# Feed-forward products on float32 operands instead of three float32r products on split operands, in an attention and feed-forward kernel

## The chip, the core and the metric

The kernel runs on one core of a Trainium2 chip. Its engines work side by side and meet through semaphores: TensorE (PE in the profile, its weight loads PEld) multiplies matrices, VectorE (DVE) and ScalarE (ACT) work on elements, GpSimd (POOL) too, and SyncE (SP) issues transfers. The metric is the time of one execution on the device in microseconds. The profile is of one execution and names instructions by engine and by the line of the kernel.

## The reference

The input is q, k and v of 8 batches, 8 heads, 576 positions and 64 features in float32. Attention is within chunks of 64 positions; its output becomes tokens of 512 features, which pass through a normalization and a feed-forward layer of 2048 hidden features (FFN):

```python
scores = scale * np.matmul(q_c, k_c.transpose(0, 1, 2, 4, 3))
scores = scores - np.max(scores, axis=-1, keepdims=True)
attn = np.exp(scores)
attn = attn / (np.sum(attn, axis=-1, keepdims=True) + 1e-09)
out = np.matmul(attn, v_c)
...
xn = (x - mu) / np.sqrt(var + 1e-06) * g_ln
ch = np.maximum(xn @ w_ch1, 0.0) @ w_ch2
return (x + ch).astype(np.float32)
```

The two weight matrices arrive as 64-bit floats.

## The kernel before

There are 4608 tokens, taken in 18 pairs of 128 (256 tokens a pair). Two pairs make a tile of 512 tokens, and there are 9 tiles.

Attention (function attention, once per pair). SP loads q and k and, later, v. PE makes the scores in 32 matmuls of 64x64 by 64 (line 159), float32, each in one of the four 64x64 quarters of the array (r is the half of the rows, c the half of the columns). DVE takes the maxima (166) and subtracts them (172), ACT takes the exponentials (176). The result is transposed, for the first four pairs by PE against an identity (191), for the others by DVE in blocks of 32 (204). PE multiplies by v in 32 more float32 matmuls (216), DVE divides (224) and takes mean and variance (234, 235), and after line 239 the tokens are transposed again, by PE (255) or DVE (267), so that features stand on the partitions.

FFN (function ffn). The weights are 16 blocks, each of 128 hidden features: 512 columns of the first matrix and 512 of the second. For a tile, up(f) makes 128 hidden features of all its tokens: four products over the 512 input features into one bank h (294). ACT applies ReLU (304). down(f) adds their share to the outputs y, one bank for each 128 tokens (317), and after the last block DVE adds the tokens (326) and SP stores them. Most products have 512 columns on the moving side; the first two tiles work for their first six blocks on single pairs, with 256 columns in up.

Precision. TensorE gets float32r operands there, which hold fewer bits than float32. So every operand is kept as two float32r tiles, the rounded value and the rest: weights wh and wl, tokens xth and xtl, activations hh and hl. A product is three matmuls, high by high, high by rest, rest by high. The rests are made by DVE: wl at line 113, hl at 305, xtl at 248 (for the first four pairs; by POOL on the same line for the others).

Weights (function convert_w, letter w in the order). A half block of 64-bit words (raw, 512 KB, line 81) is loaded; there are three buffers. ACT and four DVE instructions (89, 96, 97, 100, 104) turn it into float32 in place, ACT writes wh (108), DVE writes wl (113). After round i come the rest of half block i-1 and the load of half block i+2. There are 32 half blocks, and all are converted within the first 130 us.

Order. No scheduler decides it: the strings START, STEADY and LAST list, letter by letter, which stream (attention of a pair, FFN of a tile, conversion of weights) takes its next step, and each engine executes its instructions in that order. In the steady part PE gets up(f+1) and then down(f), so that ReLU and the rest of block f+1 have a down(f) to hide behind.

Of the kernel before, what the change touches and what calls it, by code (L numbers as in the profile page):

```python
# [7 lines left out]

F32 = mybir.dt.float32
BF16 = mybir.dt.bfloat16  # L10
F32R = mybir.dt.float32r
U32 = mybir.dt.uint32
U64 = mybir.dt.uint64
AF = mybir.ActivationFunctionType
ALU = mybir.AluOpType
AX = mybir.AxisListType

P = 128
B, H, S, D = 8, 8, 576, 64
DM = H * D  # L20
DFF = 4 * DM
T = B * S
PAIR = 2 * P
# [3 lines left out]
NK = DM // P  # L27
NF = DFF // P
NW = 2 * DM
HALF = NW // 2  # L30
RAW_AHEAD = 3
# [19 lines left out]
def chunk_attention_ffn(ctx: ExitStack, tc: tile.TileContext, qkv, g, w, out):  # L51
    nc = tc.nc
    PSUM = bass.MemoryType.PSUM

    const = ctx.enter_context(tc.tile_pool(name="const", bufs=1))
# [3 lines left out]
    xtp = ctx.enter_context(tc.tile_pool(name="xt", bufs=2))  # L59
    hp_ = ctx.enter_context(tc.tile_pool(name="hp", bufs=2))  # L60
# [9 lines left out]
    nc.gpsimd.memset(mhalf, -0.5)  # L70
    g_sb = const.tile([P, DM], F32, name="g_sb")

    wh = [const.tile([P, NW], F32R, name=f"wh{i}") for i in range(NF)]
    wl = [const.tile([P, NW], F32R, name=f"wl{i}") for i in range(NF)]

    stage, converted = {}, set()

    def fetch_w(i):
        if i < 2 * NF:
            raw = raw_pool.tile([P, HALF], U64, name="raw")  # L80
            nc.sync.dma_start(raw, w[i // 2, :, (i % 2) * HALF : (i % 2 + 1) * HALF])
            words = raw.bitcast(U32).rearrange("p (n two) -> p n two", two=2)
            stage[i] = words[:, :, 0], words[:, :, 1]

    def start_w(i):
        if i < 2 * NF:
            lo, hi = stage[i]
            wf = raw_pool.tile([P, HALF], F32, name="wf", bufs=1)
            nc.scalar.activation(wf, hi.bitcast(F32), AF.Abs)  # L89
            stage[i] = lo, hi, wf  # L90

    def round_w(i):

        lo, hi, wf = stage[i]
        wu = wf.bitcast(U32)
        nc.vector.tensor_scalar(out=wf, in0=wf, scalar1=F64_LOW, scalar2=F64_HIGH, op0=ALU.max, op1=ALU.min)
        nc.vector.tensor_scalar(  # L97
            out=wu, in0=wu, scalar1=0x07FFFFFF, scalar2=3, op0=ALU.bitwise_and, op1=ALU.logical_shift_left
        )
        nc.vector.scalar_tensor_tensor(  # L100
            out=lo, in0=lo, scalar=29, in1=wu, op0=ALU.logical_shift_right, op1=ALU.bitwise_or
        )
        start_w(i + 1)
        nc.vector.scalar_tensor_tensor(  # L104
            out=lo, in0=hi, scalar=0xC0000000, in1=lo, op0=ALU.bitwise_and, op1=ALU.bitwise_or
        )
        f, cs = i // 2, slice((i % 2) * HALF, (i % 2 + 1) * HALF)
        nc.scalar.copy(wh[f][:, cs], lo.bitcast(F32))

    def split_w(i):  # L110
        wf = stage.pop(i)[0].bitcast(F32)
        f, cs = i // 2, slice((i % 2) * HALF, (i % 2 + 1) * HALF)
        nc.vector.tensor_tensor(out=wl[f][:, cs], in0=wf, in1=wh[f][:, cs].bitcast(F32), op=ALU.subtract)  # L113
        converted.add(i)

    def convert_w():

        for i in range(RAW_AHEAD):
            fetch_w(i)
        yield  # L120
        start_w(0)
        yield
        for i in range(2 * NF):
            round_w(i)
            if i > 0:
                split_w(i - 1)
                fetch_w(i - 1 + RAW_AHEAD)
            yield
        split_w(2 * NF - 1)
        yield  # L130

    def attention(pair, xt_cols, xs, by_pe):
# [20 lines left out]
        for j in range(2):  # L153
            for a in range(HP):
                for h2 in range(2):
                    r = slice(h2 * D, (h2 + 1) * D)
                    for c in range(2):
                        cs = slice(j * P + c * D, j * P + (c + 1) * D)
                        nc.tensor.matmul(  # L159
                            s[h2][c * D : (c + 1) * D, j * HP + a, :], lhsT=q_t[r, a, cs], rhs=k_t[r, a, cs],  # L160
                            start=True, stop=True,
# [9 lines left out]
        for h2 in range(2):  # L171
            nc.vector.tensor_tensor(
                out=p_sb[:, :, h2, :], in0=s[h2], in1=top[:, :, h2 : h2 + 1].broadcast_to([P, 2 * HP, D]),
                op=ALU.subtract,
# [48 lines left out]
        for h2 in range(2):  # L223
            nc.vector.tensor_tensor(
                out=x_h[:, :, h2, :], in0=o[h2], in1=rden[:, :, h2 : h2 + 1].broadcast_to([P, 2 * HP, D]),
                op=ALU.mult,
# [14 lines left out]
            )  # L241
        yield

        xth, xtl = xt_cols()

        def rest(on, j, xt):
            js = slice(j * P, (j + 1) * P)
            on.tensor_tensor(out=xtl[:, :, js], in0=xt, in1=xth[:, :, js].bitcast(F32), op=ALU.subtract)  # L248

        if by_pe:  # L250
            xt = []
            for j in range(2):
                xt.append(bank().rearrange("p (k t) -> p k t", k=NK))
                for k in range(NK):
                    nc.tensor.transpose(out=xt[j][:, k, :], in_=xg[:, j, k * P : (k + 1) * P], identity=ident)
                nc.scalar.copy(xth[:, :, j * P : (j + 1) * P], xt[j])  # L256
                if j == 0:
                    yield
                    rest(nc.vector, 0, xt[0])
            yield  # L260
            rest(nc.vector, 1, xt[1])
        else:
            xt = work.tile([P, 2 * NK, P], F32, name="xt", tag="work")
            xg = xg.rearrange("p j (k t) -> p (j k) t", k=NK)
            for j in range(4):
                for i in range(4):
                    nc.vector.transpose(out=xt[quad(j), :, quad(i)], in_=xg[quad(i), :, quad(j)])  # L267
                yield
            for j in range(2):
                nc.scalar.copy(xth[:, :, j * P : (j + 1) * P], xt[:, j * NK : (j + 1) * NK, :])  # L270
                rest(nc.gpsimd, j, xt[:, j * NK : (j + 1) * NK, :])
        vare = small.tile([P, 2], F32, name="vare")
        nc.vector.tensor_scalar_add(vare, mv[:, :, 1], 1e-6)
        rstd = small.tile([P, 2], F32, name="rstd", bufs=6)
# [4 lines left out]
    def ffn(first, n, xt, xs, fs, last):  # L279

        nt = n * PAIR
        slots = DM // nt
        held = []
        f0, f1 = fs
        y = []

        def up(f):
            assert 2 * f in converted and all(first + i in xs for i in range(n))
            h = ps_h.tile([P, nt], F32, name="h")
            xth, xtl = xt()  # L290
            m = 0
            for k in range(NK):
                for wx, x in ((wh, xth), (wh, xtl), (wl, xth)):
                    nc.tensor.matmul(  # L294
                        h, lhsT=wx[f][:, k * P : (k + 1) * P], rhs=x[:, k, :], start=m == 0, stop=m == 3 * NK - 1
                    )
                    m += 1
            return h

        def split(f, h):  # L300
            if f % slots == 0:
                held[:] = [hp_.tile([P, slots, nt], F32R, name=f"h{i}") for i in "hl"]
            hh, hl = (x[:, f % slots, :] for x in held)
            nc.scalar.activation(hh, h, AF.Relu)  # L304
            nc.vector.scalar_tensor_tensor(  # L305
                out=hl, in0=h, scalar=0.0, in1=hh.bitcast(F32), op0=ALU.max, op1=ALU.subtract
            )
            return hh, hl

        def down(f, hh, hl):  # L310
            assert 2 * f + 1 in converted
            if f == f0:
                y.extend(ps_y.tile([P, DM], F32, name="y") for _ in range(2 * n))
            for j in range(2 * n):
                js = slice(j * P, (j + 1) * P)
                for m, (hx, wx) in enumerate(((hh, wh), (hh, wl), (hl, wh))):
                    nc.tensor.matmul(  # L317
                        y[j], lhsT=hx[:, js], rhs=wx[f][:, DM:],
                        start=f == f0 and m == 0, stop=f == f1 - 1 and m == 2,
                    )  # L320

        def finish():
            for j in range(2 * n):
                pair, jj = first + j // 2, j % 2
                x, rstd = xs[pair]
                nc.vector.scalar_tensor_tensor(  # L326
                    out=x[:, jj, :], in0=y[j], scalar=rstd[:, jj : jj + 1], in1=x[:, jj, :], op0=ALU.mult, op1=ALU.add
                )
                if last:
                    row = pair * PAIR + jj * P  # L330
                    nc.sync.dma_start(out[row : row + P, :], x[:, jj, :])

        hs = {}

        def products():
            hs[f0] = up(f0)
            yield
            for f in range(f0, f1):
                if f + 1 < f1:
                    hs[f + 1] = up(f + 1)  # L340
                    yield
                down(f, *hs.pop(f))
                hs["done"] = f + 1
                yield

        def rectified():
            for f in range(f0, f1):
                hs[f] = split(f, hs[f])
                yield
            assert hs["done"] == f1  # L350
            finish()
            yield

        return products(), rectified()
# [9 lines left out]
    class Tokens:  # L364
# [4 lines left out]

        def cols(self, i, n=1):  # L370
            if not self.x:
                self.x.extend(xtp.tile([P, NK, 2 * PAIR], F32R, name=f"xt{c}") for c in "hl")
            return [x[:, :, i * PAIR : (i + n) * PAIR] for x in self.x]

        def attention(self, i, by_pe):
            return attention(2 * self.t + i, lambda: self.cols(i), xs, by_pe)
# [54 lines left out]
```

## Time and profile before

| | us |
|---|---|
| median of 2 runs | 899.92 (899.84 to 900.0) |
| the profiled execution | 899.33 |
| its span, first to last instruction | 897.6 |
| PE busy in the span | 853.5 |
| DVE busy | 568.3 |
| ACT busy | 173.3 |
| POOL busy | 48.3 |

The granted TensorE clock is 0.997 of full speed over the span. The groups of the page that the change touches are, in us busy: matmuls of line 294 in three groups of 624 each, 236.6, 233.9 and 234.0; of line 317 in three groups of 576 each, 226.0, 224.4 and 224.4; on DVE line 305 with 101.2; on POOL line 248 with 35.6.

How to read such rows: a group has its line, engine, operation, output and inputs by name, shapes, the number of instructions, then busy time and mean duration, and behind the second bar the idle time of the engine before them and who ended it. For a matmul, "128*128 128x512" is the weights' size and the output's. Matmuls overlap, so their durations add up to more than the time they take; the distance of two starts is the rate.

### The profile page before, as it was taken

The numbers are of one execution on the slowest core, as the hardware profiler recorded it, in microseconds if no ns is written. First come the engines' busy times: TensorE is split into PE (matmuls) and PEld (weight loads), VectorE is DVE, ScalarE is ACT, GpSimd is POOL, SyncE is SP. The second block draws the span as 40 slices with busy tenths as digits, with TensorE's granted clock in tenths as the row PEclk, the third lists the DMA queues.
The fourth block names the chain that finished last, engine by engine and source line by source line (L and its number), as shares of the span: only waits on it lengthen the run. The fifth ranks groups of instructions, "written<-read, shape, count | busy, mean of one in ns | idle before, by whom it ended". The sixth has DMA issues, their size and how long they took to land.

```text
span 897.6 us, 14036 instructions
## 1 busy us (share of the span) xinstructions
PE 853.5 (95%) x5968; PEld 706.5 (79%) x5968; DVE 568.3 (63%) x1104; ACT 173.3 (19%) x301; POOL 48.3 (5%) x53
## 2 busy tenths in 40 slices
PE   2379999999999999999999999999999999999998
PEld 2368888888888788878888888888888888888886
DVE  5988887788876566656565656565666565661112
ACT  3343433412111111121212021212011111111110
POOL 0000000001000000010101010101010101010000
PEclk9999999999999999999999999999999999999999
DMA  6544153212030103010301030103010220000001
GB/s 220 191 145 161 62 175 118 94 48 71 1 135 8 48 0 119 24 47 1 119 24 47 1 118 24 47 1 117 25 47 1 72 71 1 1 30 19 0 1 47
DMA packets 20367, 55.70 MB, mean 62 GB/s; under 512 B 2256, under 2 KB 2256, under 8 KB 20304
## 3 DMA queue, kind: packets, MB, share of 16 engines
q1 hardware_dynamic: 20160, 54.53, 17.4%
q8 instruction: 47, 0.77, 0.4%
q10 hardware_dynamic: 144, 0.26, 0.1%
q14 instruction: 16, 0.13, 0.0%
HBM read 45.35 MB, written 9.44 MB: 61 GB/s over the span
## 4 chain that ended last, share of the span: by engine, by line
PE 89%; DVE 6%; DMA 2%; ACT 1%; issue 1%; SPq 0%; DVEq 0%; ACTq 0%
PE h L294 44%; PE y L317 41%; PE s L159 2%; PE s L216 2%; DMA k_t<-qkv 1%; DVE pt_sb L204 1%; DMA raw<-w 1%; DVE raw L100 1%; DVE raw L104 1%; DVE x L326 1%; DVE hl L305 1%; ACT hh L304 1%; DVE wf L97 0%; DVE top L166 0%; DVE wl L113 0%
## 5 line engine op out<-in xcount | busy, mean ns | idle before, releaser
L305 DVE SCALAR_TENSOR_TENSOR hl<-h,hh 128x512 fp32r<-128x512 f32 (+1 forms) x156 | 101.2, 650 | 264.8 <-ACT hh L304 264.6
L294 PE MATMUL h<-xth,wh 128*128 128x512 f32 (+1 forms) x624 | 236.6, 379 | 0.7 <-ACT xth L256 0.7
L294 PE MATMUL h<-xth,wl 128*128 128x512 f32 (+1 forms) x624 | 233.9, 375 | 3.0 <-DVE wl L113 3.0
L294 PE MATMUL h<-xtl,wh 128*128 128x512 f32 (+1 forms) x624 | 234.0, 375 | 1.1 <-DVE xtl L248 1.1
L317 PE MATMUL y<-wh,hh 128*128 128x512 f32 x576 | 226.0, 392 | 2.1 <-ACT hh L304 2.0
L317 PE MATMUL y<-wl,hh 128*128 128x512 f32 x576 | 224.4, 390 | 0.0
L317 PE MATMUL y<-wh,hl 128*128 128x512 f32 x576 | 224.4, 390 | 0.0
L304 ACT ACTIVATE hh<-h 128x512 fp32r<-128x512 f32 (+1 forms) x156 | 87.8, 564 | 582.5 <-PE h L294 578.9
L294 PEld LDWEIGHTS h<-xth,wl 128*128 128x128 f32 x624 | 118.6, 190 | 23.9 <-DVE wl L113 3.2
L294 PEld LDWEIGHTS h<-xth,wh 128*128 128x128 f32 x624 | 118.5, 190 | 23.2 <-ACT xth L256 1.1
L294 PEld LDWEIGHTS h<-xtl,wh 128*128 128x128 f32 x624 | 118.5, 190 | 22.0 <-DVE xtl L248 1.4
L317 PEld LDWEIGHTS y<-wh,hh 128*128 128x128 f32 x576 | 108.2, 188 | 25.1 <-ACT hh L304 3.0
L317 PEld LDWEIGHTS y<-wh,hl 128*128 128x128 f32 x576 | 108.1, 188 | 23.4 <-DVE hl L305 0.9
L317 PEld LDWEIGHTS y<-wl,hh 128*128 128x128 f32 x576 | 108.2, 188 | 21.5
L204 DVE STREAM_TRANSPOSE pt_sb<-p_sb 32x256 f32<-32x256 f32 x224 | 97.7, 436 | 5.2 <-ACT p_sb L176 1.4
L267 DVE STREAM_TRANSPOSE xt<-xg 32x256 f32<-32x256 f32 x224 | 97.6, 436 | 3.5
L248 POOL TENSOR_TENSOR xtl<-xt,xth 128x512 fp32r<-128x512 f32 x28 | 35.6, 1290 | 644.8 <-ACT xth L270 416.0
L326 DVE SCALAR_TENSOR_TENSOR x<-y,rstd,x 128x512 f32<-128x512 f32 x44 | 30.6, 749 | 15.3 <-PE y L317 15.2
L166 DVE TENSOR_REDUCE top<-s 128x8 f32<-128x512 f32 x36 | 23.2, 686 | 24.4 <-PE s L159 24.4
L89 ACT ACTIVATE wf<-raw 128x512 f32<-128x512 f32 x32 | 21.8, 683 | 76.5 <-DMA raw<-w 53.8
L159 PE MATMUL s<-k_t,q_t 64*64 64x64 f32 x1152 | 22.6, 231 | 14.1 <-DMA k_t<-qkv 14.1
L159 PEld LDWEIGHTS s<-k_t,q_t 64*64 64x64 f32 x1152 | 20.0, 144 | 19.2 <-issue 11.1
(35 smaller groups left out, 383.7 us busy)
## 6 DMA issues: line engine op xcount, KB each, us to landing
raw<-w SPq DMA_DIRECT2D x32, 512.0 KB, 3.6
q_t<-qkv SPq DMA_DIRECT2D x18, 512.0 KB, 4.2
k_t<-qkv SPq DMA_DIRECT2D x18, 512.0 KB, 5.4
v_t<-qkv SPq DMA_DIRECT2D x36, 256.0 KB, 3.1
out<-x SPq DMA_DIRECT2D x36, 256.0 KB, 2.1
g_sb<-g ACTq DMA_DIRECT2D x1, 256.0 KB, 4.5
```

The costliest lines, as they stand in the source:

```text
L89: nc.scalar.activation(wf, hi.bitcast(F32), AF.Abs)
L159: nc.tensor.matmul(s[h2][c * D : (c + 1) * D, j * HP + a, :], lhsT=q_t[r, a, cs], rhs=k_t[r, a, cs], start=True, stop=True,)
L166: nc.vector.tensor_reduce(out=top[:, :, h2], in_=s[h2], axis=AX.X, op=ALU.max)
L204: nc.vector.transpose(out=pt_sb[quad(2 * h2 + j), :, c, quad(i)], in_=p_sb[quad(2 * c + i), :, h2, quad(j)])
L216: nc.tensor.matmul(o[h2][c * D : (c + 1) * D, j * HP + a, :], lhsT=pt_sb[r, j * HP + a, c, :], rhs=v_t[j][r, a, c, :], start=True, stop=True,)
L248: on.tensor_tensor(out=xtl[:, :, js], in0=xt, in1=xth[:, :, js].bitcast(F32), op=ALU.subtract)
L267: nc.vector.transpose(out=xt[quad(j), :, quad(i)], in_=xg[quad(i), :, quad(j)])
L294: nc.tensor.matmul(h, lhsT=wx[f][:, k * P : (k + 1) * P], rhs=x[:, k, :], start=m == 0, stop=m == 3 * NK - 1)
L304: nc.scalar.activation(hh, h, AF.Relu)
L305: nc.vector.scalar_tensor_tensor(out=hl, in0=h, scalar=0.0, in1=hh.bitcast(F32), op0=ALU.max, op1=ALU.subtract)
L317: nc.tensor.matmul(y[j], lhsT=hx[:, js], rhs=wx[f][:, DM:], start=f == f0 and m == 0, stop=f == f1 - 1 and m == 2,)
L326: nc.vector.scalar_tensor_tensor(out=x[:, jj, :], in0=y[j], scalar=rstd[:, jj : jj + 1], in1=x[:, jj, :], op0=ALU.mult, op1=ALU.add)
```

## The change

FFN products are one matmul each, on operands of type float32. The second copies fall away: wl, xtl and hl, and with them the instructions that made them. The weights stay in one set of tiles ws, to which the last of the four DVE instructions writes directly; the ACT copy of line 108 is gone. Tokens are one tile xt, the activations one tile h, written by ReLU. The load of a half block is issued after each round, of half block i+3 instead of i+2. The strings of the order are untouched.

```diff
-    wh = [const.tile([P, NW], F32R, name=f"wh{i}") for i in range(NF)]
-    wl = [const.tile([P, NW], F32R, name=f"wl{i}") for i in range(NF)]
+    ws = [const.tile([P, NW], F32, name=f"ws{i}") for i in range(NF)]
...
         nc.vector.scalar_tensor_tensor(
-            out=lo, in0=hi, scalar=0xC0000000, in1=lo, op0=ALU.bitwise_and, op1=ALU.bitwise_or
+            out=ws[f].bitcast(U32)[:, cs], in0=hi, scalar=0xC0000000, in1=lo, op0=ALU.bitwise_and, op1=ALU.bitwise_or
         )
-        nc.scalar.copy(wh[f][:, cs], lo.bitcast(F32))
-
-    def split_w(i):
-        wf = stage.pop(i)[0].bitcast(F32)
-        nc.vector.tensor_tensor(out=wl[f][:, cs], in0=wf, in1=wh[f][:, cs].bitcast(F32), op=ALU.subtract)
...
             round_w(i)
-            if i > 0:
-                split_w(i - 1)
-                fetch_w(i - 1 + RAW_AHEAD)
+            fetch_w(i + RAW_AHEAD)
...
-                nc.scalar.copy(xth[:, :, j * P : (j + 1) * P], xt[:, j * NK : (j + 1) * NK, :])
-                rest(nc.gpsimd, j, xt[:, j * NK : (j + 1) * NK, :])
+                nc.scalar.copy(xt_[:, :, j * P : (j + 1) * P], xt[:, j * NK : (j + 1) * NK, :])
...
             for k in range(NK):
-                for wx, x in ((wh, xth), (wh, xtl), (wl, xth)):
-                    nc.tensor.matmul(
-                        h, lhsT=wx[f][:, k * P : (k + 1) * P], rhs=x[:, k, :], start=m == 0, stop=m == 3 * NK - 1
-                    )
-                    m += 1
+                nc.tensor.matmul(
+                    h, lhsT=ws[f][:, k * P : (k + 1) * P], rhs=x[:, k, :], start=k == 0, stop=k == NK - 1
+                )
...
             nc.scalar.activation(hh, h, AF.Relu)
-            nc.vector.scalar_tensor_tensor(
-                out=hl, in0=h, scalar=0.0, in1=hh.bitcast(F32), op0=ALU.max, op1=ALU.subtract
-            )
...
-                for m, (hx, wx) in enumerate(((hh, wh), (hh, wl), (hl, wh))):
-                    nc.tensor.matmul(
-                        y[j], lhsT=hx[:, js], rhs=wx[f][:, DM:],
-                        start=f == f0 and m == 0, stop=f == f1 - 1 and m == 2,
-                    )
+                nc.tensor.matmul(y[j], lhsT=hh[:, js], rhs=ws[f][:, DM:], start=f == f0, stop=f == f1 - 1)
```

PE in the steady part, before, at the end of an up and the start of a down (h and y are the PSUM banks, the numbers behind wh and wl count the weight tiles):

```order
L294 MATMUL h<-xth,wh_108 128x512
L294 MATMUL h<-xtl,wh_108 128x512
L294 MATMUL h<-xth,wl_124 128x512
L317 MATMUL y<-wh_107,hh 128x512
L317 MATMUL y<-wl_123,hh 128x512
L317 MATMUL y<-wh_107,hl 128x512
```

and at the same place after the change:

```order
L273 MATMUL h<-xt,ws_108 128x512 x4
L291 MATMUL y<-ws_107,h 128x512 x4
L273 MATMUL h<-xt,ws_109 128x512 x4
L291 MATMUL y<-ws_108,h 128x512 x4
L273 MATMUL h<-xt,ws_110 128x512 x4
```

An up and a down had 12 matmuls each and have 4 each; the order among them is the same.

DVE at the second half block of weights (raw words, wf the scratch tile) and the denominators of the first attention, before:

```order
L96 TENSOR_SCALAR wf<-wf 128x512
L97 TENSOR_SCALAR wf<-wf 128x512
L100 SCALAR_TENSOR_TENSOR raw<-raw,wf 128x512
L104 SCALAR_TENSOR_TENSOR raw<-raw 128x512
L113 TENSOR_TENSOR wl_112<-raw,wh_96 128x512
L182 TENSOR_REDUCE den<-p_sb 128x16
```

and after:

```order
L94 TENSOR_SCALAR wf<-wf 128x512
L95 TENSOR_SCALAR wf<-wf 128x512
L98 SCALAR_TENSOR_TENSOR raw<-raw,wf 128x512
L103 SCALAR_TENSOR_TENSOR ws_96<-raw 128x512
L171 TENSOR_REDUCE den<-p_sb 128x16
```

Each round of the weights has four DVE instructions in place of five.

SP's first transfers, before:

```order
L137 DMA k_t<-qkv 128x1024
L81 DMA raw<-w 128x512 x3
L169 DMA v_t<-qkv 128x512 x2
L81 DMA raw<-w 128x512
L137 DMA q_t<-qkv 128x1024
```

and after:

```order
L126 DMA k_t<-qkv 128x1024
L79 DMA raw<-w 128x512 x3
L158 DMA v_t<-qkv 128x512 x2
L79 DMA raw<-w 128x512 x2
L126 DMA q_t<-qkv 128x1024
```

One more block of weights stands ahead of the second pair's q and k.

More of the change, by code (lines that the diff above doesn't have):

```diff
@@ L10 @@
 BF16 = mybir.dt.bfloat16
-F32R = mybir.dt.float32r
 U32 = mybir.dt.uint32
@@ L103, in round_w @@
         start_w(i + 1)
+        f, cs = i // 2, slice((i % 2) * HALF, (i % 2 + 1) * HALF)
         nc.vector.scalar_tensor_tensor(
-            out=lo, in0=hi, scalar=0xC0000000, in1=lo, op0=ALU.bitwise_and, op1=ALU.bitwise_or
+            out=ws[f].bitcast(U32)[:, cs], in0=hi, scalar=0xC0000000, in1=lo, op0=ALU.bitwise_and, op1=ALU.bitwise_or
         )
-        f, cs = i // 2, slice((i % 2) * HALF, (i % 2 + 1) * HALF)
-        nc.scalar.copy(wh[f][:, cs], lo.bitcast(F32))
-    def split_w(i):
-        wf = stage.pop(i)[0].bitcast(F32)
-        f, cs = i // 2, slice((i % 2) * HALF, (i % 2 + 1) * HALF)
-        nc.vector.tensor_tensor(out=wl[f][:, cs], in0=wf, in1=wh[f][:, cs].bitcast(F32), op=ALU.subtract)
+        stage.pop(i)
         converted.add(i)
@@ L124, in convert_w @@
             round_w(i)
-            if i > 0:
-                split_w(i - 1)
-                fetch_w(i - 1 + RAW_AHEAD)
+            fetch_w(i + RAW_AHEAD)
             yield
-        split_w(2 * NF - 1)
         yield
@@ L242, in attention @@
         yield
[L244 to L248, printed above, removed]
+        xt_ = xt_cols()
         if by_pe:
@@ L255, in attention @@
                     nc.tensor.transpose(out=xt[j][:, k, :], in_=xg[:, j, k * P : (k + 1) * P], identity=ident)
-                nc.scalar.copy(xth[:, :, j * P : (j + 1) * P], xt[j])
+                nc.scalar.copy(xt_[:, :, j * P : (j + 1) * P], xt[j])
                 if j == 0:
                     yield
-                    rest(nc.vector, 0, xt[0])
             yield
-            rest(nc.vector, 1, xt[1])
         else:
@@ L289, in up @@
             h = ps_h.tile([P, nt], F32, name="h")
-            xth, xtl = xt()
-            m = 0
+            x = xt()
             for k in range(NK):
-                for wx, x in ((wh, xth), (wh, xtl), (wl, xth)):
-                    nc.tensor.matmul(
-                        h, lhsT=wx[f][:, k * P : (k + 1) * P], rhs=x[:, k, :], start=m == 0, stop=m == 3 * NK - 1
-                    )
-                    m += 1
+                nc.tensor.matmul(
+                    h, lhsT=ws[f][:, k * P : (k + 1) * P], rhs=x[:, k, :], start=k == 0, stop=k == NK - 1
+                )
             return h
@@ L301, in split, with down @@
             if f % slots == 0:
-                held[:] = [hp_.tile([P, slots, nt], F32R, name=f"h{i}") for i in "hl"]
-            hh, hl = (x[:, f % slots, :] for x in held)
+                held[:] = [hp_.tile([P, slots, nt], F32, name="h")]
+            hh = held[0][:, f % slots, :]
             nc.scalar.activation(hh, h, AF.Relu)
-            nc.vector.scalar_tensor_tensor(
-                out=hl, in0=h, scalar=0.0, in1=hh.bitcast(F32), op0=ALU.max, op1=ALU.subtract
-            )
-            return hh, hl
-        def down(f, hh, hl):
+            return (hh,)
+        def down(f, hh):
             assert 2 * f + 1 in converted
@@ L371, in cols @@
             if not self.x:
-                self.x.extend(xtp.tile([P, NK, 2 * PAIR], F32R, name=f"xt{c}") for c in "hl")
-            return [x[:, :, i * PAIR : (i + n) * PAIR] for x in self.x]
+                self.x.append(xtp.tile([P, NK, 2 * PAIR], F32, name="xt"))
+            return self.x[0][:, :, i * PAIR : (i + n) * PAIR]
         def attention(self, i, by_pe):
```

## The prediction

> **What bounds the kernel now.** I read the first two parts of the page, then the stretches of the span, then the chain of work that ended last.
>
> ```profile
> PE 853.5 (95%) x5968; PEld 706.5 (79%) x5968; DVE 568.3 (63%) x1104; ACT 173.3 (19%) x301; POOL 48.3 (5%) x53
> PE   2379999999999999999999999999999999999998
> DVE  5988887788876566656565656565666565661112
> PEclk9999999999999999999999999999999999999999
> 0.00:39.20 39.20, 10.57 (x208) 8.73 (x208) 28.36 (x52) 13.46 (x21) 0.74 (x7) 1.00 0.60 218
> 39.20:130.00 90.80, 81.39 (x833) 71.62 (x834) 79.34 (x154) 35.29 (x68) 2.88 (x4) 0.98 0.39 136
> 130.00:893.00 763.00, 760.99 (x4928) 626.09 (x4928) 459.23 (x899) 124.54 (x213) 44.67 (x42) 1.00 0.13 44
> PE 89%; DVE 6%; DMA 2%; ACT 1%; issue 1%; SPq 0%; DVEq 0%; ACTq 0%
> ```
>
> The three rows of stretches give PE, PEld, DVE, ACT and POOL busy, the clock, the DMA share and GB/s. There are two regimes. Up to 39.2 us PE idles 28.6 us while DVE is 28.36 us busy converting weights; up to 130 us PE idles another 9.4 us and DVE is nearly full (79.34 of 90.8). From 130 to 893 us PE idles 2 us of 763, and DVE has over 300 us to spare. So 85% of the span goes by the rate at which PE takes matmuls, and what the change does to that rate is almost the whole answer. A busy PE here is a modelled time with overlap, so the rate must be read from starts.
>
> ```profile
> L317 PE MATMUL y<-wh,hh 128*128 128x512 f32 x576 | 226.0, 392 | 2.1 <-ACT hh L304 2.0
> L294 PE MATMUL h<-xth,wh 128*128 128x512 f32 x528 | 207.7, 393 | 0.0
> L294 PE MATMUL h<-xth,wh 128*128 128x256 f32 x96 | 28.9, 301 | 0.7 <-ACT xth L256 0.7
> 441.21 0.39 PE L317 MATMUL y<-wh,hh 128*128 128x512 f32 x1
> ...
> 446.65 0.39 PE L317 MATMUL y<-wh,hh 128*128 128x512 f32 x1
> 68.25 0.28 PE L294 MATMUL h<-xth,wh 128*128 128x256 f32 x1
> ...
> 68.85 0.28 PE L294 MATMUL h<-xth,wl 128*128 128x256 f32 x1
> ```
>
> The two rows at 441.21 and 446.65 are 24 matmuls apart: 5.44/24 = 226.7 ns for one float32r matmul of 512 columns. The next two are 5 apart: 0.60/5 = 120 ns for 256 columns. The difference is 106.7 ns for 256 columns, 0.4167 ns a column, and what is left, 226.7 - 213.3 = 13.3 ns, is fixed per matmul. (The page prints f32 for float32r operands of matmuls; lines 294 and 317 are float32r.) A product is three such matmuls: 680 ns at 512 columns, 360 ns at 256. There are 576 + 528 = 1104 products of the first kind and 96 of the second.
>
> **The price of a float32 product.** No row shows a float32 product of 128x128 by 512. The attention has float32 products of 64x64 by 64, and the transposes are float32.
>
> ```profile
> L159 PE MATMUL s<-k_t,q_t x1152: 218/218/366, 6.6 to 757.8; 64*64 64x64 f32 x192
> 452.19 1.16 PE L216 MATMUL s<-v_t,pt_sb 64*64 64x64 f32 x64
> L216 PE MATMUL s<-v_t,pt_sb x64: 218/218/267, 452.2 to 453.1; 64*64 64x64 f32 x64
> 107.31 1.03 PE L255 MATMUL s<-ident,xg 128*128 128x128 f32 x8
> L255 PE MATMUL s<-ident,xg x8: 270/272/273, 107.3 to 108.1; 128*128 128x128 f32 x8
> ```
>
> The loops around line 159 make 2 x 4 x 2 x 2 = 32 matmuls for each of 18 attentions, 576; the trace has 1152. So each float32 product leaves two matmul records, each with a weight load. The 64 of one attention take (1.16 - 0.218)/63 = 14.95 ns each; they go in turn to the four 64x64 quarters of the array (the code's r and c), so a quarter takes a record every 59.8 ns. At 0.4167 ns a column, 64 columns once are 26.7 ns and twice 53.3 ns. Twice fits, with 6.5 ns left over. The transposes, 128 columns: (1.03 - 0.272)/7 = 108.3 ns, twice 128 columns is 106.7, 1.6 left over. These paces alone could also be a weight load of 64 or 128 columns that sets the pace, because the shapes are square. The durations of single records tell more, best early, where PE's clock is low.
>
> ```profile
> L159 PE MATMUL s<-k_t,q_t x64: 311/311/366, 6.6 to 8.2; 64*64 64x64 f32 x64
> L191 PE MATMUL s<-ident,p_sb x8: 421/421/445, 11.8 to 13.3; 128*128 128x128 f32 x8
> 60.13 0.42 PE L294 MATMUL h<-xth,wh 128*128 128x256 f32 x1
> 60.35 0.42 PE L294 MATMUL h<-xtl,wh 128*128 128x256 f32 x1
> L294 PE MATMUL h<-xtl,wh x3: 415/415/416, 60.4 to 61.6; 128*128 128x256 f32 x3
> ```
>
> There a float32r matmul of 256 columns comes every 0.22 us, about the columns' 106.7 ns doubled, 0.833 ns a column, and lasts 415 ns. A float32 transpose of 128 columns lasts 421 ns, as long as 256 columns. A float32 product record of 64 columns lasts 311 ns, 104 less than 415, which is 125 columns less than 256: it is as long as 131 columns. So a float32 record passes its columns twice, and a product, with two records, four times. At the higher clock the same reading is looser: 272 ns against 283 for 256 columns, and 218 where one pass would give 203 and two 230.
>
> A record of 512 columns then takes 1024 x 0.4167 = 426.7 ns plus a fixed part of 1.6 (transposes), 6.5 (attention products) or 13.3 (float32r). I take 6.5: that row is nearest, both float32 and a true product. Record 433.2, product 866.3, against 680: +186.3 ns. At 256 columns: 2 x (213.3 + 6.5) = 439.7 against 360: +79.7 ns. Sum: 1104 x 186.3 = 205.7, and 96 x 79.7 = 7.7, together **+213.3 us**. With 1.6 ns: +201.6. With 13.3 ns: +229.8. One matmul in the code in place of three is thus more PE time, not less.
>
> **What the other edits give.**
>
> ```profile
> L113 DVE TENSOR_TENSOR wl<-raw,wh 128x512 fp32r<-128x512 f32 x32 | 21.9, 685 | 0.0
> L248 DVE TENSOR_TENSOR xtl<-s,xth 128x512 fp32r<-128x512 f32 x8 | 5.4, 686 | 0.0
> L305 DVE SCALAR_TENSOR_TENSOR hl<-h,hh 128x512 fp32r<-128x512 f32 (+1 forms) x156 | 101.2, 650 | 264.8 <-ACT hh L304 264.6
> L108 ACT CAST wh<-raw 128x512 fp32r<-128x512 f32 x32 | 20.9, 654 | 3.5 <-DVE raw L104 3.0
> sum 130.00, DVE 13.01; mean DVE 3.25
> sum 130.00, DVE 5.40 POOL 0.00; mean DVE 1.35 POOL 0.00
> sum 130.00, DVE 9.07; mean DVE 4.54
> 0.00:39.20 39.20, 3.42 (x5) 1.00 0.60 218
> PE h L294 <- DVE wl L113: 3.0, 1, 3.0
> PE h L294 <- DVE xtl L248: 1.1, 1, 1.1
> PE s L191 <- DVE xtl L248: 3.0, 2, 1.9
> ```
>
> After 130 us the remainders hl (DVE), xtl (POOL) and their reads cost and give nothing: PE does not wait for them (2 us idle in all), and it gets slower, so the cover grows. ReLU at line 304 stays, has a whole set of products in front of it, and no product waits for DVE any more. Before 130 us it matters. The rows with sums are, in that stretch, the wl of line 113 (13.01 us), the DVE's xtl of line 248 (5.40 us) and the hl of line 305 (9.07 us); the row under them is line 113 up to 39.2 us. Up to the first product at 39.2 us five wl (3.42 us) and one xtl (0.69 us) fall out of a busy DVE: 4.1 us. After it PE waited 3.0 + 1.1 + 3.0 = 7.1 us for the removed wl and xtl. I take **-11.2 us**. At most it is all that DVE loses there, 13.0 + 5.4 + 9.1 = 27.5 us. At worst it is a loss: the fetch of a weight block moves one round earlier and, on SP's queue, one more block of 512 KB stands ahead of the second q and k; at the 218 GB/s of that stretch this is 2.4 us, for which line 159 would wait. The ACT copies of line 108 go too; ACT is 35.29 us busy of 90.8 and hides them.
>
> The profiled execution took 899.3 us, its span 897.6 and 1.7 around it; the median of the runs is 0.6 higher. Sum: 899.3 + 213.3 - 11.2 = **1101 us**. Bounds: 899.3 + 201.6 - 27.5 = 1073 and 899.3 + 229.8 + 2.4 = 1132.
>
> **Rivals.** (a) It gets faster. Each record passes its columns once, and what set 59.8 and 108.3 ns was the weight load. Then a product is 2 x 226.7 = 453.3 ns: 1104 x -226.7 = -250.2, 96 x -120 = -11.5, time 899.3 - 261.7 - 11.2 = 626 us; if loads are as long as their 128 columns and not hidden, 2 x (53.3 + 213.3 + 6.5) = 546 ns and about 738 us. It decides where a record of 512 columns is under 340 ns. For it: square shapes hide the difference in the paces. Against it: 421 and 311 ns at the low clock.
> The Trainium skill has a page on each side. Its page TensorE: Matmul & The Clock Gate (Part 2, what each phase is for, and Back-to-back issue gap) says that columns stream at one per cycle and gives N/2.4 + 2.5 ns with no word on the operands' type; an estimate by that is 2 x 215.8 = 431.7 ns a product and about 600 us. Its page FP8 and Floating Point Precision (TensorE Precision Notes) says that true FP32 takes four passes; with that the low-clock durations agree, and by it alone, four times 213.3 ns with nothing fixed, the sum would be about 1086 us.
>
> (b) The fixed part comes with each pass, not each record: 4 x 226.7 = 907 ns. 1104 x 226.7 + 96 x 120 = 261.7; 899.3 + 261.7 - 11.2 = 1150 us. Against it: 1.6 and 6.5 ns left over after two passes.
>
> (c) The second weight load of a product can't be hidden.
>
> ```profile
> L255 PEld LDWEIGHTS s<-ident,xg x8: 138/139/142, 107.1 to 108.0; 128*128 128x128 f32 x8
> L317 PEld LDWEIGHTS y<-wh,hh x8: 187/188/188, 441.0 to 448.5; 128*128 128x128 f32 x8
> ```
>
> If each record paid 139 ns more, a product would be 1144 ns: 1104 x 464.3 + 96 x 357.6 = 547, and 1435 us. Against it: transposes come every 108.3 ns although their loads last 139, so loads overlap the matmul ahead, and float32 loads are no longer than float32r's 188.
> The Trainium skill speaks against the change here: TensorE: Matmul & The Clock Gate (Weight-path perf modes) says that the quick weight load is off for FP32 operands, and its LDWEIGHTS formula gives 128/1.2 = 107 ns; two of them unhidden would, as an estimate, make about 1360 us, hidden ones change nothing. The 139 ns rows show no such slowing of float32 loads.
>
> **How the numbers follow.** The four passes as summed: 0.83. (a) 0.06, (b) 0.08, (c) 0.03. The time is that of the likeliest, 1101 us. Its own range is 1073 to 1132; taking in (b), 1073 to 1152, leaves out some 0.1 to 0.2. A measurement of this kernel tells about 2% from no change, 18 us; (a) alone is faster, nothing here lands within 2%, all else is slower: 0.06, 0.00, 0.94.
>
> **What the next profile would show.** The two products' lines with two records for each product, 1152 for y and 1248 for h, some 433 ns apart at 512 columns; 230 or less would be (a), 454 (b), 570 (c). DVE busy down by 128 us (101 hl, 22 wl, 5 xtl), to about 440, and PE without a wait after 130 us. The first product some 4 us before 39.2. If PE waits in the long stretch for ACT's ReLU or for a transfer, or if the clock row drops under four-pass work, the sum is wrong in a place that I have put at nothing.

## The result, and the profile after

The changed kernel takes 1083.99 us (2 runs, 1083.7 to 1084.27) against 899.92 before: slower by 184 us, ratio 1.2045 (95% interval 1.1994 to 1.2097). A second comparison, of three rounds, gave 1.2047 (1.2029 to 1.2066).

First the page of the changed kernel, its busy times and slices, then three stretches of its span (columns: PE, PEld, DVE, ACT and POOL busy with the number of instructions, granted clock, DMA share, GB/s).

```profile
span 1082.5 us, 11356 instructions
PE 1052.7 (97%) x4768; PEld 504.2 (47%) x4768; DVE 450.2 (42%) x908; ACT 151.4 (14%) x269; POOL 13.3 (1%) x25
PE   3899999999999999999999999999999999999998
DVE  6775543484544445352616153535444453510001
PEclk8799999999999999999999999999999999999999
0.00:33.79 33.79, 10.33 (x208) 8.54 (x209) 23.49 (x44) 9.93 (x15) 0.74 (x7) 0.79 0.73 258
33.79:130.00 96.21, 93.80 (x699) 64.25 (x700) 62.48 (x117) 27.12 (x54) 2.88 (x4) 0.95 0.40 137
130.00:1078.00 948.00, 948.00 (x3863) 431.46 (x3861) 362.86 (x748) 114.40 (x200) 9.64 (x14) 1.00 0.10 34
```

The long stretch, where before PE idled 2 us of 763, is now 948 us long and PE idles not at all. DVE's 459 us of work there are 363. The first FFN product starts at 33.8 us instead of 39.2, and between it and 130 us PE idles 2.4 us instead of 9.4. The two groups of products and some of their starts follow; a row with a count merges that many matmuls from the first start to the last end.

```profile
L273 PE MATMUL h<-xt,ws 128*128 128x512 f32 (+1 forms) x1248 | 523.2, 564 | 0.7 <-ACT xt L240 0.7
L291 PE MATMUL y<-ws,h 128*128 128x512 f32 x1152 | 520.7, 595 | 0.0
L291 PEld LDWEIGHTS y<-ws,h 128*128 128x128 f32 x1152 | 218.6, 191 | 263.6 <-issue 261.4
L291 PE MATMUL y<-ws,h x1152: 592/593/1058, 42.4 to 1078.0; 128*128 128x512 f32 x192
501.60 6.60 PE L291 MATMUL y<-ws,h 128*128 128x512 f32 x15
L273 PE MATMUL h<-xt,ws x34: 379/379/483, 61.8 to 75.0; 128*128 128x256 f32 x34
68.29 3.62 PE L273 MATMUL h<-xt,ws 128*128 128x256 f32 x16
```

576 products of y leave 1152 records, 624 of h leave 1248: two each, with a weight load for each. At 512 columns a record comes every (6.60 - 0.593)/14 = 429 ns, at 256 every (3.62 - 0.379)/15 = 216 ns. The difference, 213 ns for 256 columns, is 0.833 ns a column, twice the 0.4167 of a float32r matmul. What is left over is 429 - 426.7, some 2.5 ns a record. A product takes 858 ns instead of 680: 1104 x 178.5 = 197 us, and 96 x (432 - 360) = 7 us. **PE's rate accounts for +204 us, 20 more than the +184 that were measured.** What has to be found is where these 20 us were saved. (Starts are read to 0.01 us, so the 204 are known to 1 or 2 us.)

### The profile page after: what moved, and what is told of

Same layout as the page of the kernel before. It is cut to its first block, busy times and chain, and to the rows that moved or that the text cites. A ratio compares the mean times of both kernels' runs of the same rounds, so it can differ in the third digit from the quotient of the medians.

```text
span 1082.5 us, 11356 instructions
## 1 busy us (share of the span) xinstructions
PE 1052.7 (97%) x4768; PEld 504.2 (47%) x4768; DVE 450.2 (42%) x908; ACT 151.4 (14%) x269; POOL 13.3 (1%) x25
## 4 chain that ended last, share of the span: by engine, by line
PE 96%; DVE 2%; DMA 1%; ACT 0%; issue 0%; SPq 0%
PE h L273 46%; PE y L291 46%; PE s L148 2%; PE s L205 2%; DMA k_t<-qkv 1%; PE s L239 0%; DVE raw L98 0%; DVE top L155 0%; DVE ws L103 0%; PE s L180 0%; DVE p_sb L161 0%; DVE wf L95 0%; ACT xt L240 0%; DVE wf L94 0%; DVE xg L228 0%
## 5 line engine op out<-in xcount | busy, mean ns | idle before, releaser
L273 PE MATMUL h<-xt,ws 128*128 128x512 f32 (+1 forms) x1248 | 523.2, 564 | 0.7 <-ACT xt L240 0.7
L291 PE MATMUL y<-ws,h 128*128 128x512 f32 x1152 | 520.7, 595 | 0.0
L273 PEld LDWEIGHTS h<-xt,ws 128*128 128x128 f32 x1248 | 236.8, 192 | 257.0 <-issue 250.0
L291 PEld LDWEIGHTS y<-ws,h 128*128 128x128 f32 x1152 | 218.6, 191 | 263.6 <-issue 261.4
L282 ACT ACTIVATE h<-h 128x512 f32<-128x512 f32 (+1 forms) x156 | 88.0, 564 | 868.2 <-PE h L273 855.6
L213 DVE TENSOR_TENSOR x<-s,rden 128x512 f32<-128x512 f32 x36 | 23.2, 685 | 121.4 <-PE s L205 121.4
L94 DVE TENSOR_SCALAR wf<-wf 128x512 f32<-128x512 f32 x32 | 13.3, 416 | 32.4 <-ACT wf L87 32.3
L228 DVE SCALAR_TENSOR_TENSOR xg<-x,mv,g_sb 128x512 f32<-128x512 f32 x36 | 25.0, 735 | 0.0
L223 DVE BATCH_NORM_STATS2 stats<-x 128x6 f32<-128x512 f32 x36 | 24.4, 678 | 0.6
L161 DVE TENSOR_TENSOR p_sb<-s,top 128x512 f32<-128x512 f32 x36 | 23.3, 680 | 0.0
L98 DVE SCALAR_TENSOR_TENSOR raw<-raw,wf 128x512 uint32<-128x512 uint32 x32 | 22.2, 693 | 1.1
```

The lines of the kernel that those rows point to most:

```text
L161: nc.vector.tensor_tensor(out=p_sb[:, :, h2, :], in0=s[h2], in1=top[:, :, h2 : h2 + 1].broadcast_to([P, 2 * HP, D]), op=ALU.subtract,)
L223: nc.vector.bn_stats(out=stats, in_=x[:, j, :])
L228: nc.vector.scalar_tensor_tensor(out=xg[:, j, :], in0=x[:, j, :], scalar=mv[:, j, 0:1], in1=g_sb, op0=ALU.subtract, op1=ALU.mult)
L273: nc.tensor.matmul(h, lhsT=ws[f][:, k * P : (k + 1) * P], rhs=x[:, k, :], start=k == 0, stop=k == NK - 1)
L291: nc.tensor.matmul(y[j], lhsT=hh[:, js], rhs=ws[f][:, DM:], start=f == f0, stop=f == f1 - 1)
```

## The experiments

Each is timed in three rounds against the kernel before on the same chip (898.7 to 898.9 us there); the first product's start is from the run's trace.

| run | us | ratio to before (95%) | first product at |
|---|---|---|---|
| e1, one float32 product, rests made | 1092.2 | 1.2146 (1.2128 to 1.2164) | 38.5 us |
| e2, three float32r, no rests | 883.3 | 0.9825 (0.9809 to 0.9842) | 36.4 us |
| e3, changed kernel, late fetch | 1083.9 | 1.2057 (1.2037 to 1.2078) | 33.4 us |
| e4, changed kernel, late fetch, wl | 1086.8 | 1.2096 (1.2076 to 1.2116) | 36.0 us |
| e5, three bfloat16, rests made | 859.4 | 0.9564 (0.9549 to 0.9579) | 38.9 us |
| e6, the same, wl by POOL | 857.9 | 0.9546 (0.9528 to 0.9565) | 38.2 us |
| e7, changed kernel and xtl | 1086.7 | 1.2085 (1.2065 to 1.2106) | 34.6 us |
| e8, changed kernel again | 1082.6 | 1.2047 (1.2029 to 1.2066) | 33.6 us |
| e9, three float32r, rests made, unread | 898.2 | 0.9995 (0.9985 to 1.0005) | 38.4 us |

### The two halves of the change taken apart (e1, e2)

e1 makes the products as the changed kernel does, and all the rests as the kernel before:

```diff
-F32R = mybir.dt.float32r
+F32R = mybir.dt.float32
...
-                for wx, x in ((wh, xth), (wh, xtl), (wl, xth)):
...
+                nc.tensor.matmul(
+                    h, lhsT=wh[f][:, k * P : (k + 1) * P], rhs=xth[:, k, :], start=k == 0, stop=k == NK - 1
+                )
...
-                for m, (hx, wx) in enumerate(((hh, wh), (hh, wl), (hl, wh))):
...
+                nc.tensor.matmul(y[j], lhsT=hh[:, js], rhs=wh[f][:, DM:], start=f == f0, stop=f == f1 - 1)
```

> One float32 matmul per product, but the rests wl, xtl and hl are still made as before (with the ACT copy and the later fetch), and read by no product. In the traces PE's rate accounts for +204 us (1104 x 178.7 ns and 96 x 72 ns), and the change came out 19 us better than that. Theory A: the 19 us come from the DVE work that is gone in the first 130 us, so with the work back it is lost again: 1097 to 1106 us, first product near 39 us. Rival B: they come from PE being slower, which covers DVE's work; then the rests cost little: 1084 to 1090 us.

e2 is the other half, the changed kernel with float32r tiles, an ACT copy that writes the weights, and each matmul issued three times:

```diff
+        nc.scalar.copy(ws[f][:, cs], lo.bitcast(F32))
...
+            for m in range(3 * NK):
+                k = m // 3
+                nc.tensor.matmul(
+                    h, lhsT=ws[f][:, k * P : (k + 1) * P], rhs=x[:, k, :], start=m == 0, stop=m == 3 * NK - 1
+                )
...
+                for m in range(3):
+                    nc.tensor.matmul(
+                        y[j], lhsT=hh[:, js], rhs=ws[f][:, DM:],
+                        start=f == f0 and m == 0, stop=f == f1 - 1 and m == 2,
+                    )
```

> Three float32r matmuls per product at 226.7 ns each, all three on the high halves; the rests are neither made nor added, so the products have float32r's precision and three times the size. Theory A: without the rests' DVE work 19 us go whatever PE's rate is: 876 to 884 us against 899.9. Rival B: with PE at the quick rate DVE stays the one waited for in the first 130 us, and less than 11 us go: 889 us or more.

Measured: e1 1092.2, between the two theories; e2 883.3, as theory A had it. So neither theory alone is right. Without the rests 15.4 us go at the quick rate (898.7 to 883.3). About 1 us of this is clock: e2's runs were granted 0.999 to 1.0 and most of the kernel before 0.997, and its two at 1.0 took 897.5 and 897.7. At the slow rate 8 to 10 us go (1092.2 in e1 against 1084.0 and 1082.6 of the changed kernel, which also lacks e1's ACT copy).

And the slow rate by itself costs 1092.2 - 898.7 = 193.5 us where all rests are still made, 10.5 less than the 204 of PE's records, although the other engines do all that they did. Where no rests are made it costs more: 883.3 to 1082.6 and 1084.0 are 199 to 201 us, and there the first product comes 2.6 to 2.8 us earlier than in e2, so that from the first product on 202 to 203 of the 204 us are paid. So it is waits caused by the rests that a slower PE covers.

The 2.6 to 2.8 us belong to the ACT copy of the weights. e2 keeps it and the changed kernel does not; before the first product the two differ in nothing else but the types that it and its neighbours write. PE's wait just before the first product, in e2 and in the changed kernel:

```profile
PE h L276 <- ACT xt L242: 3.1, 1, 3.1
PE h L273 <- ACT xt L240: 0.7, 1, 0.7
```

The waits of PE in e1 (us in total, times, longest) show part of the 10.5 us:

```profile
PE s L255 <- DVE p_sb L172: 6.9, 1, 6.9
PE s L159 <- DMA k_t<-qkv: 6.8, 1, 6.8
PE s L159 <- DVE raw L100: 6.6, 1, 6.6
PE s L191 <- ACT p_sb L176: 3.3, 1, 3.3
PE s L191 <- DVE xtl L248: 3.2, 3, 1.6
PE s L255 <- DVE xtl L248: 2.9, 1, 2.9
PE s L255 <- DVE xg L239: 2.5, 1, 2.5
PE s L216 <- ACT pt_sb L193: 0.8, 1, 0.8
PE h L292 <- ACT xth L256: 0.7, 1, 0.7
PE y L313 <- ACT hh L301: 0.2, 1, 0.2
130.00:1085.00 955.00, 954.79 (x3887) 435.25 (x3886) 465.83 (x909) 128.76 (x219) 44.04 (x42) 1.00 0.11 36
```

The last row answers one question at once: with hl back on DVE and xtl back on POOL (44.04 us), PE idles 0.2 us of 955 after 130 us, so at the slow rate the rests cost nothing there. In the same view of the kernel before there are four rows that e1 lacks or has nearly lost:

```profile
PE h L294 <- DVE wl L113: 3.0, 1, 3.0
PE y L317 <- ACT hh L304: 2.0, 3, 0.9
PE s L216 <- DVE pt_sb L204: 2.0, 6, 0.3
PE h L294 <- DVE xtl L248: 1.1, 1, 1.1
```

The waits of the attention's first steps are about the same in both. These four add up to 8.1 us before and 0.2 in e1; others grow, and all rows together are 39.8 us before and 33.9 in e1. But e1 changes two things there: PE is slower, and no product reads a rest any more, so that the rows with wl and xtl could be gone for that reason alone. One more run tells them apart.

### Rests made and not read, at the quick rate (e9)

The kernel before with all three matmuls of a product on the high halves:

```diff
-                for wx, x in ((wh, xth), (wh, xtl), (wl, xth)):
+                for wx, x in ((wh, xth), (wh, xth), (wh, xth)):
...
-                for m, (hx, wx) in enumerate(((hh, wh), (hh, wl), (hl, wh))):
+                for m, (hx, wx) in enumerate(((hh, wh), (hh, wh), (hh, wh))):
```

> The kernel before with all its rests still made, but with the three float32r matmuls of a product all on the high halves, so that no product reads a rest and the output is three times the float32r product. PE has its quick rate. The run with one float32 product and all rests made came out 10.5 us better than PE's rate says. Theory A: a slower PE hides waits; then here, at the quick rate, little goes: 895 to 899 us. Rival B: there the products no longer had to wait for rests; then it shows here too: 886 to 891 us.

Measured: 898.16 us, ratio 0.9995 (0.9985 to 1.0005). No gain: theory A. That products no longer read the rests is worth nothing by itself at the quick rate (no run has the slow rate with the rests read); the waits of PE in e9 show why.

```profile
PE s L191 <- DVE xtl L248: 3.6, 3, 1.9
PE s L255 <- DVE xg L239: 3.2, 1, 3.2
PE y L317 <- ACT hh L304: 2.1, 3, 1.0
PE s L216 <- DVE pt_sb L204: 2.0, 6, 0.3
```

The rows of wl and xtl ahead of products are gone here too, and PE waits for the same busy DVE a little later, at the transposes (xg, 3.2 us, which the kernel before lacks and e1 has with 2.5). The rows of hh and pt_sb, 4.1 us, are still there at the quick rate and 0.2 us at the slow one. So the 10.5 us belong to the slower PE, which covers what the making of the rests holds up. The row of pt_sb shows how. It is one wait in each of six attentions after 140 us; here is one of them in the kernel before, DVE's part and then PE's:

```profile
307.77 0.69 DVE L305 SCALAR_TENSOR_TENSOR hl<-h,hh 128x512 fp32r<-128x512 f32 x1 [1.09 <-ACT hh L304]
308.50 1.81 DVE L204 STREAM_TRANSPOSE pt_sb<-p_sb 32x256 f32<-32x256 f32 x4
309.69 0.34 PE L216 MATMUL s<-v_t,pt_sb 64*64 64x64 f32 x6
310.36 1.14 PE L216 MATMUL s<-v_t,pt_sb 64*64 64x64 f32 x58 [0.33 <-DVE pt_sb L204]
```

DVE waits for ReLU, makes hl, and only then does the last four transposes, to 310.31 us. PE came to the products by v at 309.69. They take 1.81 us from the first start to the last end; where nothing is waited for it is 1.16, as in e2, which makes no hl:

```profile
297.99 1.16 PE L207 MATMUL s<-v_t,pt_sb 64*64 64x64 f32 x64
```

So a wait that the rows give as 0.33 us is worth 0.65, because the modelled end of the matmul ahead covers much of the rest, and six of them are 3.9 us. In e1 the same four transposes, behind hl there too, end at 362.37 us, just in time for the slower PE:

```profile
360.56 1.81 DVE L204 STREAM_TRANSPOSE pt_sb<-p_sb 32x256 f32<-32x256 f32 x4
362.47 1.16 PE L216 MATMUL s<-v_t,pt_sb 64*64 64x64 f32 x64
```

All waits of PE add up to 39.4 us in e9 and 33.9 in e1, 5.5 less, and the six are worth 1.9 more than their rows. That names 7.4 of the 10 us between the two kernels; what the other 2 to 3 are made of is not settled, and the 204 are not known much better. e2's list of waits has a row neither of hh nor of DVE's pt_sb, so without the rests these waits are gone at the quick rate too.

### Which of the removed instructions counted (e3, e4, e7, e8)

e3 is the changed kernel with the fetch in its old place:

```diff
-            fetch_w(i + RAW_AHEAD)
+            if i > 0:
+                fetch_w(i - 1 + RAW_AHEAD)
```

> The changed kernel with the fetch of weight blocks in its old place, half block i+2 after round i. Theory: the earlier fetch was worth little, as PE and DVE wait for q and k and for each other: 1084 to 1087 us. Rival: the earlier fetch gave a quarter or more of the 19 us: 1089 us or more.

Measured 1083.9 (ratio 1.2057, 1.2037 to 1.2078), against 1.2047 for the changed kernel: no difference. The earlier fetch is worth nothing that can be measured, in either direction.

e4 is e3 with the wl subtraction back on DVE:

```diff
+    def split_w(i):
+        wf = stage.pop(i)[0].bitcast(F32)
+        f, cs = i // 2, slice((i % 2) * HALF, (i % 2 + 1) * HALF)
+        nc.vector.tensor_tensor(out=wl, in0=wf, in1=ws[f][:, cs], op=ALU.subtract)
...
             if i > 0:
+                split_w(i - 1)
                 fetch_w(i - 1 + RAW_AHEAD)
```

> The changed kernel with one more DVE subtraction for each weight half block (the wl instruction, into a scratch tile that nothing reads) and the old fetch place; no xtl and no hl. 32 x 0.69 us of DVE work, 13 us of it in the first 130 us. Theory A (DVE's work there is on the path): 1092 to 1098 us. Rival B (covered by the slower PE): under 1088 us.

Measured 1086.8: rival B, 3 us dearer than e3, though the two intervals touch. The first product comes 2.6 us later (36.0 against 33.4 us), and five of the 32 wl, 3.4 us, stand before it. So most of what wl costs fits the delay of the first product, and the other 27 cost little.

e7 puts the DVE's xtl back, and nothing else:

```diff
+        def rest(j, xt):
+            js = slice(j * P, (j + 1) * P)
+            nc.vector.tensor_tensor(out=xtl, in0=xt, in1=xt_[:, :, js], op=ALU.subtract)
...
+                    rest(0, xt[0])
             yield
+            rest(1, xt[1])
```

> The changed kernel with the eight DVE subtractions of xtl back (first four pairs, into a scratch tile that nothing reads), nothing else. All rests together cost 1092.2 - 1083.9 = 8.3 us over the changed kernel with the late fetch, wl alone 3.0 us; 5.3 us are left for xtl and hl. Theory: they are xtl's, because it reads the bank that PE's next transposes wait for and stands on DVE ahead of work that PE waits for: 1087 to 1090 us. Rival: they are hl's, 101 us on DVE: 1085 us or less.

> The changed kernel itself on the same chip as the run with xtl, so that the two can be compared: 1084 us, ratio to before 1.2045.

Measured 1086.7 for e7 and 1082.6 for e8 on the same chip: 4.1 us for eight instructions of 0.69 us, with intervals that touch (1086.7 is just under the 1087 to 1090 that I expected, which was set against 1083.9). The first product comes 1.0 us later. The rows of PE's waits in e7 that e8 does not have are these two:

```profile
PE s L181 <- DVE xtl L238: 2.1, 2, 1.1
PE s L245 <- DVE xtl L238: 1.7, 1, 1.7
```

They are 3.8 us: PE's next transposes write the bank that xtl still reads. Other waits shrink, and all rows together are 28.0 us against 25.3. So 3.0 (wl) + 4.1 (xtl) = 7 of the 8 to 10 us are named; what hl and e1's ACT copy add is the difference of 1 to 3 us and lies within the intervals.

### Another type for the three matmuls (e5, e6)

A record of float32 has 2.5 ns beside its columns, a float32r matmul 13.3. If that belongs to the type, three matmuls of a type without it are quicker than both kernels. e5 is the kernel before with bfloat16 high halves and rests (and without the bitcasts of the high halves).

```diff
-F32R = mybir.dt.float32r
+F32R = mybir.dt.bfloat16
```

> The kernel before with bfloat16 in place of float32r for the high halves and the rests, three matmuls per product; fewer bits are kept of every operand. Theory: one pass of 512 columns takes 213.3 ns plus a fixed part; if the fixed 13.3 ns belong to float32r alone and bfloat16 has the 2.6 ns of a float32 record, a product takes 648 ns instead of 680: 1104 x -32 and 96 x -32 = -38 us, 862 us. Rival: the fixed part goes with three changing weight tiles, not with the type: 899 us, no change.

e6 moves wl to POOL as well:

```diff
-        nc.vector.tensor_tensor(out=wl[f][:, cs], in0=wf, in1=wh[f][:, cs], op=ALU.subtract)
+        nc.gpsimd.tensor_tensor(out=wl[f][:, cs], in0=wf, in1=wh[f][:, cs], op=ALU.subtract)
```

> As the run with bfloat16, and the rests wl are made by POOL instead of DVE, which takes 13 us of work out of DVE's first 130 us. If DVE's work there is on the path, 5 to 12 us less than with wl on DVE; if POOL, at 1.3 us for an instruction of this size, comes too late for the products, as slow or slower.

Measured: e5 859.4, ratio 0.9564 (0.9549 to 0.9579), 39.5 us under the kernel before and near the 862 of the theory. Matmuls of line 317 in e5, and below them a stretch of line 276 in e2, where each product is three float32r matmuls on the same weight tile:

```profile
439.77 0.38 PE L317 MATMUL y<-wh,hh 128*128 128x512 bf16 x1
...
444.95 0.38 PE L317 MATMUL y<-wh,hh 128*128 128x512 bf16 x1
L317 PEld LDWEIGHTS <-hh x10: 98/98/98, 440.2 to 445.6; 128*128 128x128 bf16 x10
```

```profile
443.13 2.88 PE L276 MATMUL h<-xt,ws 128*128 128x512 f32 x12
```

24 matmuls from 439.77 to 444.95 are 215.8 ns each, 2.5 beside the columns. In e2 it is (2.88 - 0.389)/11 = 226.5 ns as in the kernel before, so the 13.3 ns go with float32r and not with changing weight tiles. Nor do they come from the longer weight load: at 256 columns a float32r matmul comes every 120 ns with the same 13.3 beside its columns, while its loads last 190. e6, with 13 us taken off DVE's first 130 us, is 857.9, less than the 5 to 12 us below e5 that were expected if DVE's work is on the path; its interval overlaps that of e5, so no gain is shown. POOL needed 37.8 us for the 32 subtractions, and the first product came at 38.2 instead of 38.9 us.

## Why the prediction was right, and where it was off

- **Two records, two passes each.** Right: 1152 and 1248 records, 0.833 ns a column. The rivals fall by the rows above: (a) would have had 227 ns a record, (b) 454, (c) 570; it is 429, and a load of 190 ns hides in it (PEld 47% busy). This is what the float32 durations at the low clock had said, 421 and 311 ns. (The granted clock reads 0.50 from 59.3 to 62.6 us, where the row of 415 ns is, but 1.00 from 6 to 14 us, where those two are; that the clock was low there too is inferred from durations alone, 421 ns against 272 for the same kind of transpose later.) The Trainium skill's four passes for true FP32 (FP8 and Floating Point Precision, TensorE Precision Notes) agree with it, at 0.833 ns a column in each of two records. The Trainium skill's rule that the quick weight load is off for FP32 (TensorE: Matmul & The Clock Gate, Weight-path perf modes) agrees with the loads of 98 ns for bfloat16 and 190 for float32, but float32r's 188 are no shorter, and no row shows PE waiting for a load; the prediction had only these two types to compare, and so saw no slowing.
- **The fixed part of a record.** Too large: I took 6.5 ns from the attention's products, and it is 2.5, near the 1.6 of the transposes. The attention's 6.5 came from four quarters of the array in turn, which is not what a full-size product does; the row with the same size of weights was the nearer one. That is 213 against 204 us, 9 us too many.
- **Rests after 130 us cost and give nothing.** Right at the slow rate: PE idles 0.2 us of 955 in e1 with them and 0 of 948 without. Not at the quick rate of the kernel before: the "2 us idle in all" that the prediction set aside are the six waits behind hl, which are worth 3.9 us, and they go.
- **The saving, -11.2.** Too small, and this is the step that was off beside the fixed part. It was added up from waits at the quick rate, and at that rate the rests are worth 15.4 us (e2), the six waits after 130 us among them. The ACT copies, of which the prediction said that ACT hides them, are worth 2.6 to 2.8 more. That is 18 of the 20 us, and the first product came 5.4 us earlier instead of 4.1. The bound of 2.4 us for the earlier fetch was not needed (e3).
- **PE's slower rate, charged in full.** Nearly right for a kernel without rests, 202 to 203 of 204 us from the first product on (e2 against the changed kernel). With the rests made it is not: there the slower PE covers 10.5 us of the waits that they cause (e1), and e9 shows that it is the rate and not the missing reads. "The cover grows" was right, then, but it gives nothing on top of the saving. The 10.5 us and the 15.4 us are in part the same waits, and the sum must count them once: 204 - 15.4 less 2.6 to 2.8 is 186, 204 - 10.5 less 8 to 10 is 184 to 185, both within 2 us of the +184.
- **DVE busy.** 450 us against the 440 forecast. The busy time of an engine counts overlapping instructions once, so taking out groups of 128 us in total can lower it by less; no run was made to show that this is all.

The two errors, 9 us and about 9 us (20 against 11.2), have the same sign; 1101 became 1084.

## What to carry to other kernels

Count what one instruction in the code becomes in the trace, and read the rate from starts, before taking three matmuls against one: here one float32 product costs 3.8 float32r matmuls. Where the shapes of the known instruction can't tell a slow pass from a slow weight load, single durations at another clock can. When the bounding engine is made slower and other engines lose work in the same change, count each wait once: with the rests still made the slower PE covered 10 of its 204 us, and with them gone there was hardly anything left to cover. And look up what a small idle time is made of before setting it aside: 2.0 us of waits in the rows were 3.9 us of the span here.

## What was not expected of the hardware

A float32r matmul of 512 columns comes every 226.7 ns and a bfloat16 one every 215.8, with 13.3 and 2.5 ns beside the columns; a float32 record has 2.5 too. For three matmuls a product that is 33 ns of 680, and bfloat16 made the whole kernel 4.4% faster than the kernel before.
